# Rotating every filter group in float32 in place, and building the sine arguments on GpSimd, in a gated recurrence with a long convolution

## The chip, the cores and the metric

The kernel runs on one core of a Trainium2 chip. The metric is the device time of one execution in microseconds. Three runs of the kernel before gave 459.9, 460.58 and 461.4 us; the median is 460.58 us. The engines are called as in the profile: PE (TensorE, matrix products; PEld is its weight loading), DVE (VectorE), ACT (ScalarE), POOL (GpSimd) and SP (SyncE, which here only issues DMA transfers).

## The reference

Input `x` and `f_logit` have shape (4, 6272, 256): four sequences of 6272 steps with 256 channels. The first part is a gated linear recurrence, the second a convolution over the whole sequence between two projections, with multiplicative gates:

```
f = lower_bound + (1 - lower_bound) * sigmoid(f_logit);  i = 1 - f
h[t] = f[t] * h[t-1] + i[t] * x[t]                       # for all t
x1, x2, x3 = split(h @ w_proj, 3)                        # 256 -> 3 x 256
conv = irfft(rfft(x2, axis=time) * rfft(filter_fft, axis=time))   # circular, length 6272
out = (x1 * conv * x3) @ w_out
```

The filter is (6272, 256) and is the same for all four sequences, so its spectrum is needed once.

## The kernel before

The length 6272 is split as 49 x 128, and the transforms are done as two small dense transforms by matrix products. The tables for them (`D1`, `FT`, `VA`, `VB`, `ID`) are sines of arguments that are worked out on the chip from index tables.

**Stages.** `prepare` loads the filter, turns it into a spectrum and stores that in DRAM (`H`, 16 units). `hgrn(b)` loads `x` and `f_logit` of sequence b in 13 chunks, applies the sigmoid (ACT, L337), multiplies (POOL, L339), transposes on PE (L351), makes the gate (L364 or L366) and scans (DVE, L372) into `HA`. A copy of the beginning of `HA` behind its end, called a wrap, is made by ACT, POOL or a DMA (L301). `spectrum(b)` projects (`phase_p`, L725), does the first transform (L737), the second (L795), multiplies with the filter's spectrum (L816, L825) and goes back (L835). `gate(b)` forms x1 * x3 (L400, L422, L431); `phase_o(b)` finishes the inverse (L869), multiplies (L875), projects with `w_out` (L887) and stores. The projection of a batch reads every scan of that batch.

**The filter's way.** The 49 rows of 128 x 256 come in 13 groups: twelve of four rows (512 KB each) and one of a single row. Group g is loaded into a scratch place (`raws`: parts of the tiles X2, Hu and HA that later hold other things). A matrix product with a rotated identity, `rot`, turns each row by its own amount (`rotate`, L637); the result lies in two PSUM banks and is copied into the tile `f2` by ACT or DVE (operation `f2`, L291 or L296). All 13 copies must be there before the first transform of the filter, `FF1` (L661), which is followed by `afs` copies, `FF2` (L679), `hw` copies and stores (`hst`) for each of 16 units.

Before the change, six groups (`PLAIN`: 0, 2, 4, 6, 8, 10) are rotated as float32 straight from where the DMA put them. The other seven are first cast to float32r by ACT or POOL (operation `fr`) into one of two tiles (`afs` and `Hx`), and rotated from there. `rot` is a float32r tile that the plain groups read as float32.

**The sine arguments.** POOL writes eight index tables with iota (L512). DVE makes eleven columns of constants (one value a partition), multiplies and adds (L534, L537, L552), and folds the arguments into one period with two tensor-by-scalar passes and a subtraction (`fold`, L520 to L522), in two halves: `args0` for columns 0 to 519, `args1` for 520 to 1031. ACT takes the sine of each half (L563). Warming matmuls (`warm`, L603) fill gaps on PE.

**Order.** The functions do not issue anything; they record some 2,400 operations with what they read and write. The string `ORDER` then lists them all: three characters give the operation's number, its engine, and its PSUM bank. So the order on every engine, the choice of the engine, SP's queue of DMA issues and the PSUM banks are written out by hand (by an offline search that used the costs in the code). Each engine works through its list in order. An operation that must wait holds everything behind it on its engine. Eight PSUM banks of 512 float32 are shared by all; a rotation takes two, and a bank is free again when the copy that reads it has run.

```
def rotate(e, pb, r0=r0, rn=rn, fr=fr, turner=turner):
    pr = PS[:, pb:pb + 2].rearrange("m a (r e) -> m (a r) e", e=256)
    for r in range(r0, r0 + rn):
        nc.tensor.matmul(pr[:, r - r0, :], turner[:, m0_of(r):m0_of(r) + 128],
                         fr[:, r - r0, :], start=True, stop=True)
```

Of the kernel before, what the change touches and what calls it, by code (L numbers as in the profile page):

```python
# [21 lines left out]
S = 6272  # L22
# [13 lines left out]
PLAIN = (0, 2, 4, 6, 8, 10)  # L36
# [28 lines left out]
class Plan:  # L65
# [63 lines left out]
    "AAYBIgBFgAMYABIAgVACIA+gAkWBBgAhTBMgAvVAZVBWgArRBTgA9YANIAfRADgAiTAcSBPgBJAApXBKSAbQBLCBGQA/VBogBCYBagAPIAOABdgBHA"  # L129
    "BNSBhgBAFBkgBDWBOCDwgBUQAEYBXYDxgBEGARIEIgBQYAmVD8gBVABYVASIAlUATYBRTBZFD9gAVYAUIAdRAoQBbQBSLEJgBeABfSBcAEUgBiWBgK"  # L130
    "EVgBlAAeVBjOAQABmQBpAAxSBnAAqSBsYBqUAsXBrMAuXAFgBwUBuQAWYBxMB3WDyABvIB1UB4GBzSB2MByYDzYB+QEKAB0KB6UCAWB/AB7MD+ACFQ"
    "B5YD0SCBOCGACHUD1CD/YD4QCIED2KCDWEggD5ACKUB9gCEGD6IEhgEASELYCLEEEWEBKEsgEFGAjVECKCOQEtgEWAAtUAwUCCYCJYCVUAXYEGOCPA"
    "CXSCWEEMQAHACYKEQWEXYAJACQSE4gEROENAAyUE5gAaUCRKEiAESOCTSAIAAYYEYUCUCEOIEcWAKAFCgCeSCSYEZMEdGFDgEjYCgQCfCEeOChACaS"
    "EuACnQEaMEkWCZYCbCEvYCoIClUElGCjSE6AEmOEoQFMgCmECiYE7YEpIFNgCkCEwUEqICwWExEE0SCxGEyMCqQFXgETYE1CC1WErgCpYCrAEPYFWg"
    "E2KE8UEbYCNgFEAE/QC2OC3SFhgFAAFFYE9MCuWFggC4CCdgFBICvGAGgFOACzWE+MFGSCyYC0GC5YFPYFJQFHKC+UFqgFKAFIKEngC6WC/EFrgC7G"
    "FQUFLICtgDASFYADHWFRMAnRDBCFTQFSMDIGDCYDFSFZYF0gFUADQWB8gDGCFVIDDUFiAC9gDKSDEMFaQDRGDJYFjYDLCDXWFbIDVUALADNgDOSDYO"
    "DWEF1gFcIDPCFdWD7YFsADTUMTgDSYFeOCcgFkQDUEFtYDgSFfOFlAFnUDhCFmIDeWMfgFoEC8gDaSD3YDfGCMgFpMFuQEDYDbCMggDlWDZYCsgEfY"
    "F2AFvIDMgDnUDiYDmGEzYF+gDjSFwIDoEBtYFxWDkCE3YJQUFyODqQDpYJSEF3YFzOJRVDrAEHYJVSJWTJTFDsgF4QF7WJYDF5IDtgDuUJUYF8OJXC"
    "F6IF/gMUgJaTF9OGigJbQJZYJcDGIRJdIG0gDvEGQWJeYGJBG9gGUUGRGGGQDdgGVEGKSGHIMhAGAWGLCGOQGBOGMUGPAGrgGCSDcgGNEMrgGEQGDK"
    "MVAGSWGFAGWSGTOJfVGXCJgXJkRJlQJhFJmJGYTJnAJivGeVGZDJoYJpQJjYGfNJqXJuRJsHGaSJrIJwBGjWGbCJtYGcUGnuJvRGdEJzTJxpJ0QGoY"  # L140
    "J1DJ4XJyYJ2IGgSGsUJ6HGhKJ3YG1QGwEGluJ5XG5AHGSGkYJ7vGxYGmYJ9VHQgHHCJ+RGusJ8YGpWJ/FHMSGvYGqGG3oGtYHZgG+UG2YG6YKABHIW"
    "HNKG4YGyQHJGHAsHKSGzAKBYHigG7WHLCMsgHCsHBYKCQG/YMiYKEAHORHRTHDYHrgHPJMtAKDQHVrHERHTDKHVKFoG8GHWYHUYKITHFJKGYKMQKJF"
    "HaWKOAKKrH0UHeuKLYH4QHSYH+gH1EHbYHXSHcuHfYMuYHjUHYCHlsH5AHdYIHgH2WHgSH3GHnsHmYHkYHsQMWYHhCH6WHuoHoYIQgHpUH7GH/SHwo"
    "HvYHqEH8WKNQIBCH9OIIUHxYHtYIZgIDqIAYIRRIKEICYHyWITBKPoIEYKRTHzGIMsKQYKSUIiQKTDILYIsgIFWINYIjAKUsKWTIVpKVYKXVIGGMXQ"
    "IJYI1gKZFIUYKYLIWYIaWMYAMbUIeGMZIIOSM3gMcEM4gKbXISYIPCIfYMdMIXQKdHImSIYAIcuMjUInCIkQKaYMkMIdYJHgIoWIlAI+gKcTMlMIbY"
    "KgSIpGItQKerKiCIqUMnWIvoKfYIxAKhTNDgMoGIyYIgRIrMNEgIwYM5AMpOKlQI2UIhBKjrMvWI3YKnAIuYI6sKkYMzSM6YMwGKmRNQgI4EMxOKqQ"
    "I7YNPgM0CIzUKsAM1KM7WI0EJAYI5YNFAKrUKopKvSKtsKpYM8GM/QKuYKxCJIUNGYM9ONbgNAAI8SNcgJMEMygNBIKwXJKEK0WI9CI/UJLYKyvK2G"
    "K1RJBsKzYNHSK3BNRAK5WJDsJCYK4YNLQNICNlgK7OJEYJFUNMANSYNmgNJKK6XJGEK+WNdANNIK/SNTTJJYLAGNeYK8vNXQNUDLBqK9YLDVNvgNYA"
    "NVLLEWLCYNwgLFFLIXLKHLJVJNYLGuNnANfSLLtLHYLNWNZILMYLOXLPGNiUNgCLQvN5gJOQNjENhKLRYNoYNOgRtXJPAN6gRuWM+gNkMRvHLSQRwG"
    "LXSNxALTINpUNsWNqENyYLYKLUQODgNtGOEgNrMLZSLVAMeYNuOLcULWgLaCNaYNzQLdMLbgRyXN0ALhSR0HN1IN7AN2ULmWONgN3ELiKN8YOOgLeQ"  # L150
    "OFAN4MLjSLfALnOOGYLrULkCN9QLsMOAWN+ALoSMqAOXgN/IOYgOBGLlgOHULpCNKgOCOLwQOPAOKSLxILtWUwgOLCOQYLqgOIEOMKLyQLuGOJMLzA"
    "L1WORSOZAL2OL0gRzROSCOaYLvgL6UR1BNWYOTKOUQMaYObWM2YU8gL7MOVAL3SOcGNCAOdOOeUMmAOWIVJgL8WL4CVIgUxgOfMMEQL9GU9gOgML/S"
    "LggMFIOxUL5gL+gMAKOhQOyEOtWOiAOvTOuOUyAO3QOwDOjWO4AOnTUzYOkOVKAO1QOoDOpWO2AOlUU+AOzQOmMOrSU/YO0AMBUOsKOqGMJQMCEVLY"
# [43 lines left out]
def kernel(  # L197
# [241 lines left out]
    def prepare(head, tmp):  # L439
# [79 lines left out]
        def fold(a, b):  # L519
            ts(v[:, a:b], in0=w[:, a:b], scalar1=1.0 / S, scalar2=big, op0=AOP.mult, op1=AOP.add)  # L520
            ts(v[:, a:b], in0=v[:, a:b], scalar1=-big, scalar2=float(S), op0=AOP.add, op1=AOP.mult)
            dve.tensor_tensor(v[:, a:b], w[:, a:b], v[:, a:b], op=AOP.subtract)  # L522
# [455 lines left out]
```

## Time and profile before

| What | Value |
|---|---|
| median of three runs | 460.58 us |
| the profiled execution: its time, and its span on the core | 461.27 us, 459.3 us |
| PE busy | 444.2 us, 97% of the span |
| PE's weight loads | 346.6 us, 75% |
| DVE busy | 402.4 us, 88% |
| ACT busy | 406.7 us, 89% |
| POOL busy | 306.0 us, 67% |
| DMA moved | 121.40 MB, mean 264 GB/s |
| TensorE clock granted | 0.999 |

A row of groups reads: line, engine, operation, out<-in by tile names, shapes, xcount | busy us in total, mean ns of one | idle time of the engine just before, and what ended it. A row in order of time reads: start us, duration us, engine, line, operation, tiles, shapes, xcount [idle before <-releaser]. In the chain of waits, each row is a start, a duration and what it was. A busy PE means that matmuls are in flight, not that it runs at its peak. A line such as L291 or L296 is that of the helper `copy`, which many operations share; there the tile names tell what it is.

### The profile page before, as it was taken

How to read it: one execution, taken by the hardware profiler on the slowest of the kernel's cores; microseconds unless marked ns; L12 is line 12 of the kernel's file. 1: busy time of each engine (PE TensorE's matmuls, PEld its weight loads, DVE VectorE, ACT ScalarE, POOL GpSimd, SP SyncE). 2: the span in 40 equal slices, each digit the busy share in tenths (PEclk: the TensorE clock that was granted, in tenths of full speed). 3: DMA queues.
4: the chain of work that ended last, by engine and by line, in shares of the span. 5: the costliest groups of instructions: out<-in, count | busy, mean ns of one | idle time of the engine just before them, and what ended most of it. 6: DMA issues, size and time to landing. Idle time of an engine off the chain costs nothing.

```text
span 459.3 us, 14604 instructions
## 1 busy us (share of the span) xinstructions
PE 444.2 (97%) x6009; PEld 346.6 (75%) x6009; DVE 402.4 (88%) x450; ACT 406.7 (89%) x563; POOL 306.0 (67%) x282
## 2 busy tenths in 40 slices
PE   8999999999999999999999999999999999999996
PEld 6777777767766889878667789766768897777794
DVE  8389996699999995899999997999999976999873
ACT  6899999998999989989998978899999978898664
POOL 5399786288898743878897535979886504979500
PEclk9999999999999999999999999999999999999999
DMA  8999999848897998367769788399789750856077
GB/s 321 387 349 330 316 340 407 314 143 253 272 310 248 337 326 298 106 233 265 279 229 296 284 294 350 101 320 326 226 244 304 287 229 26 241 185 186 31 289 290
DMA packets 45154, 121.40 MB, mean 264 GB/s; under 512 B 4384, under 2 KB 8352, under 8 KB 45088
## 3 DMA queue, kind: packets, MB, share of 16 engines
q1 hardware_dynamic: 45088, 120.47, 75.2%
q8 instruction: 47, 0.77, 0.7%
q14 instruction: 19, 0.16, 0.1%
HBM read 86.12 MB, written 31.98 MB: 257 GB/s over the span
## 4 chain that ended last, share of the span: by engine, by line
PE 66%; DVE 15%; ACT 6%; DMA 5%; issue 5%; POOL 2%; ACTq 0%; SPq 0%; DVEq 0%; POOLq 0%
PE PS L400 15%; PE PS L725 9%; PE PS L835 9%; PE PS L887 7%; PE PS L351 6%; DVE HA L372 6%; PE PS L795 6%; PE PS L737 6%; DVE ys L875 4%; DMA FL<-in_f_logit_dram 3%; PE PS L869 2%; PE PS L661 2%; DVE PP L816 2%; DMA X<-in_moe_filter_fft_dram 1%; ACT fTs L364 1%
## 5 line engine op out<-in xcount | busy, mean ns | idle before, releaser
L339 POOL TENSOR_TENSOR XT<-XT,FL 128x1024 f32<-128x1024 f32 (+1 forms) x49 | 109.8, 2245 | 53.6 <-ACT FL L337 36.5
L372 DVE TENSOR_TENSOR_SCAN HA<-fTs,HA,PS 128x512 f16<-128x512 f32 (+1 forms) x96 | 112.9, 1201 | 2.8 <-ACT fTs L364 2.0
L400 PE MATMUL PS<-HA,W 128*128 128x490 f16 (+1 forms) x416 | 103.8, 367 | 1.0 <-DVE HA L372 0.3
L825 POOL TENSOR_TENSOR PP<-HA,Hu 98x1008 f16<-98x1008 f16 x39 | 81.8, 2106 | 6.8 <-ACT HA L291 2.7
L291 ACT CAST HA<-PS 128x1024 f16<-128x1024 f32 (+1 forms) x98 | 79.1, 833 | 4.2 <-PE PS L737 2.2
L431 POOL TENSOR_TENSOR zt<-gx 128x490 f16<-128x490 f32 (+1 forms) x43 | 52.4, 1223 | 41.1 <-ACT gx L291 16.6
L816 DVE TENSOR_TENSOR PP<-PS,Hu 98x1008 f16<-98x1008 f32 x57 | 66.7, 1199 | 0.6 <-ACT gx L293 0.5
L875 DVE TENSOR_TENSOR ys<-PS,zt 128x1024 fp32r<-128x1024 f32 (+1 forms) x52 | 58.7, 1149 | 8.5 <-PE PS L869 6.7
L887 PE MATMUL PS<-Wo,ys 128*128 128x256 f32 x392 | 58.1, 293 | 0.6 <-DVE ys L875 0.3
L364 ACT ACTIVATE fTs<-PS,cc 128x512 f32<-128x512 f32 (+1 forms) x84 | 55.3, 679 | 2.8 <-PE PS L351 2.1
L835 PEld LDWEIGHTS <-PP 98*128 98x128 f16 x1024 | 50.2, 97 | 9.8 <-issue 1.7
L400 PEld LDWEIGHTS <-W 128*128 128x128 f16 x416 | 34.4, 97 | 30.6 <-issue 7.8
L835 PE MATMUL PS<-VV,PP 98*128 98x98 f16 x1024 | 55.9, 206 | 0.3
L887 PEld LDWEIGHTS PS<-Wo,ys 128*128 128x128 f32 x392 | 49.7, 188 | 6.0 <-DVE ys L875 1.5
L293 ACT ACTIVATE gx<-PS 128x490 f32<-128x490 f32 (+1 forms) x87 | 50.1, 583 | 4.5 <-PE PS L400 3.1
L291 ACT CAST Th<-PS 128x784 f16<-128x784 f32 x59 | 48.4, 820 | 4.1 <-PE PS L835 3.1
L337 ACT ACTIVATE FL<-FL 128x1024 f32<-128x1024 f32 (+1 forms) x49 | 49.4, 1010 | 1.8 <-DMA FL<-in_f_logit_dram 1.6
L351 PE MATMUL PS<-iden,FL 64*128 64x64 f32 x736 | 42.7, 231 | 2.5 <-ACT HA L293 0.9
L725 PE MATMUL PS<-W,HA 128*128 128x256 f16 x392 | 44.6, 273 | 0.2
L725 PEld LDWEIGHTS <-HA 128*128 128x128 f16 x392 | 43.0, 142 | 1.2 <-issue 0.2
L351 PEld LDWEIGHTS PS<-iden,FL 64*128 64x128 f32 x736 | 31.7, 138 | 16.0 <-issue 2.6
L422 DVE TENSOR_TENSOR zt<-PS,gx 128x490 f16<-128x490 f32 (+1 forms) x61 | 38.8, 647 | 1.6 <-PE PS L400 0.9
(128 smaller groups left out, 741.8 us busy)
## 6 DMA issues: line engine op xcount, KB each, us to landing
FL<-in_f_logit_dram SPq DMA_DIRECT2D x45, 512.0 KB, 5.8
XT<-in_x_dram SPq DMA_DIRECT2D x45, 512.0 KB, 6.3
Hu<-H SPq DMA_DIRECT2D x39, 512.0 KB, 4.9
out_dram<-osb SPq DMA_DIRECT2D x22, 512.0 KB, 4.5
out_dram<-PP SPq DMA_DIRECT2D x16, 512.0 KB, 5.6
Hx<-H SPq DMA_DIRECT2D x13, 512.0 KB, 4.3
out_dram<-HA SPq DMA_DIRECT2D x10, 512.0 KB, 5.0
X<-in_moe_filter_fft_dram SPq DMA_DIRECT2D x9, 512.0 KB, 7.4
```

The lines of the kernel that those rows point to most:

```text
L291: nc.scalar.copy(dst, src)
L339: op("u", {"POOL": 0.1 + 0.553 * nb}, lambda e, xt=xt, ft=ft: nc.gpsimd.tensor_tensor(xt, xt, ft, op=AOP.mult), r=[("ft", k)], w=[("xt", k)])
L351: nc.tensor.transpose(bank(pb)[:, at[p] + j:at[p] + hn:nb], src[ps, j, cols], iden[ps, ps])
L364: nc.scalar.activation(fT, sT, AF.Identity, scale=by, bias=1.0)
L372: nc.vector.tensor_tensor_scan(h, fT, bank(pb)[:, 512 - hn:512 + hn], init, op0=AOP.mult, op1=AOP.add),
L400: nc.tensor.matmul(PS[:, p, 0:n], W13[:, kh, js], HA[:, HB[kh] + t0:HB[kh] + t0 + n], start=(kh == 0), stop=(kh == 1))
L725: nc.tensor.matmul(pp[:, r - r0, :], column(HB[kh], q_of(r)), W2[:, kh, :], start=(kh == 0), stop=(kh == 1))
L816: nc.vector.tensor_tensor(pr, px.unsqueeze(1).broadcast_to([TB, 2, UE, 63]), hh, op=AOP.mult)
L825: nc.gpsimd.tensor_tensor(pr, spec[:, o, :, 1:64].unsqueeze(1).broadcast_to([TB, 2, UE, 63]), hh, op=AOP.mult)
L835: nc.tensor.matmul(PS[:, ib + o, pr * TB:(pr + 1) * TB], PP[:TB, k, o, n, 2 * pr:2 * pr + 2, :], v[:TB], start=(n == 0), stop=(n == 1))
L875: nc.vector.tensor_tensor(late["ys"][:, yk, :, 0:rn * 128], PS[:, cb:cb + 2, 0:rn * 128], late["zt"][:].rearrange("p k r m -> p k (r m)") ...
L887: nc.tensor.matmul(po[:, i, :], late["ys"][:, yk, kh, i * 128:(i + 1) * 128], Wo[:, kh, :], start=(kh == 0), stop=(kh == 1))
```

## The change

1. `PLAIN` and the casts `fr` are gone. All 13 groups are rotated from where the DMA put them, as float32, and `rot` is a float32 tile. The cost written for a rotation, from which the order was searched, is 0.12 us a row for all of them, where it was 0.43 for a plain row and 0.12 for a cast one.
2. Three index tables are left of eight. The offsets that the other five held are now immediate scalars, so the five multiply-adds of the first half become eleven shorter ones.
3. The constant columns become an operation of their own on DVE (`cols`); both halves of the arguments run on POOL, in the order that is written.
4. `ORDER` is new throughout. On POOL the arguments stand behind the padding of `f2` and ahead of the table work. On ACT the list starts with the copy of group 0, the sine of the first half, and the copies of groups 2, 4, 6 and 3; the sine of the second half comes next. PE rotates groups 0, 1, 2, 4, 6, 5, 3, 8, 9, 7, 10, 12, 11; ACT runs the table load and first sigmoid after the copy of group 10, while DVE copies 12 and 11. Elsewhere some dozens of copies change engines, and wraps move to SP's queue: 27 of 48 are on it after, 18 before.

```diff
-PLAIN = (0, 2, 4, 6, 8, 10)
...
-        rot = tmp.tile([128, 256], F32R, name="rot")
+        rot = tmp.tile([128, 256], F32, name="rot")
...
-                    (128, [[0, 2], [49, 2], [98, 32]], 0), (128, [[1568, 2], [0, 64]], 1568),
-                    (98, [[0, 2], [2304, Q]], 0),
-                    (98, [[1568, 2], [0, Q]], 1568), (98, [[1568, 2], [0, Q]], 0),
-                    (98, [[-1568, 2], [0, Q]], 1568), (98, [[-1568, 2], [0, Q]], 3136),
-                    (256, [[49, 256]], 0)):
+                    (128, [[0, 2], [49, 2], [98, 32]], 0), (98, [[0, 2], [2304, Q]], 0), (256, [[49, 256]], 0)):
...
+        def folded(e):
+            g = pool if e == "POOL" else dve
+            def fold(a, b):
+                g.tensor_scalar(v[:, a:b], in0=w[:, a:b], scalar1=1.0 / S, scalar2=big, op0=AOP.mult, op1=AOP.add)
+                g.tensor_scalar(v[:, a:b], in0=v[:, a:b], scalar1=-big, scalar2=float(S), op0=AOP.add, op1=AOP.mult)
+                g.tensor_tensor(v[:, a:b], w[:, a:b], v[:, a:b], op=AOP.subtract)
+            return g, fold
...
-            stt(w[:, 0:128], in0=cD, scalar=prow[:], in1=oD, op0=AOP.mult, op1=AOP.add)
-            for i, k in enumerate((kre, kre, k2, k2)):
-                stt(w[:, 128 + 98 * i:226 + 98 * i], in0=cF, scalar=k,
-                    in1=oF[i], op0=AOP.mult, op1=AOP.add)
...
+        def args0(e):
+            g, fold = folded(e)
+            g.memset(cD[:, 64:65], 3136)
+            for at, n, c, k, o in [(0, 64, cD[:, 0:64], prow[:], 1568.0), (64, 1, cD[:, 64:65], prow[:], 1568.0),
+                                   (65, 63, cD[:, 65:128], prow[:], 3136.0)] + [
+                    (128 + 98 * i + Q * j, Q, cF[:, Q * j:Q * j + Q], k, o[j]) for i, (k, o) in enumerate((
+                        (kre, (1568.0, 3136.0)), (kre, (0.0, 1568.0)), (k2, (1568.0, 0.0)), (k2, (3136.0, 1568.0))))
+                    for j in range(2)]:
+                g.tensor_scalar(w[:, at:at + n], in0=c, scalar1=k, scalar2=o, op0=AOP.mult, op1=AOP.add)
+            fold(0, 520)
+
+        def args1(e):
+            g, fold = folded(e)
+            for i, (k, o) in enumerate(((kk, ore), (kim, oim))):
+                g.tensor_scalar(w[:, 520 + 256 * i:776 + 256 * i], in0=cI, scalar1=k, scalar2=o,
+                                op0=AOP.mult, op1=AOP.add)
             fold(520, 1032)
...
-            op("args", {"DVE": c}, fn, r=st + ["pint", "rot"] + ["cols0"] * i, w=[f"cols{i}", f"v{i}"])
+        op("cols", {"DVE": 1.7}, colset, r=["pint", "rot"], w=["cols1"])
+        for i, (fn, a, b, c, p) in enumerate(((args0, 0, 520, 4.5, 5.5), (args1, 520, 1032, 3.2, 3.2))):
+            op("args", {"DVE": c, "POOL": p}, fn, r=st + ["pint", "rot", "cols1"], w=[f"v{i}"])
...
-            if g in PLAIN:
-                fr, ft, turner = raw, et, rot[:].bitcast(F32)
-            else:
-                j = g // 2 % 2
-                fr, ft, turner = afs[j]...., [("af", j, 0), ("af", j, 1)], rot
-                op("fr", {"ACT": 0.08 + 0.214 * rn, "POOL": 0.1 + 0.235 * rn, "DVE": 0.1 + 0.267 * rn},
-                   lambda e, raw=raw, fr=fr, rn=rn: copy(e, fr[:, 0:rn], raw[:, 0:rn]), r=et, w=ft)
...
-            rt = op("rot", {"PE": (0.43 if g in PLAIN else 0.12) * rn}, rotate, r=ft + ["rot"], take=2)
+            rt = op("rot", {"PE": 0.12 * rn}, rotate, r=et + ["rot"], take=2)
```

More of the change, by code (lines that the diff above doesn't have):

```diff
@@ L134 @@
[L134 to L153, printed above, removed]
@@ L189 @@
[L189 to L192 removed]
+    "AAYA/gBCgAMYABIAaVACIBFgAbSBLgAuRBOgAnXA+YANIArSBRgAeTBIgAdSBXgAcUApQAwVAxXAOYBAWBBGBDQBEIBGSBjgBagBMQBUgBdgBggAQY"
@@ new lines @@
+    "APADqgBSVBHCDrgBNABPTBTFAvRD2gBQLAUYAsQECgBJQAWYATID3gBYWBKAAVIAyTARAADgAtVASIAzRBZGBbTEDgAXYBVQBcDBeWEOgBWABkSBhU"
+    "BlKAqTBiMBfGAiQAhQAgXAfTEPgAlRBoQBqSDsABvUBrKBxWBpABwMBtSBsYByGDtYD4AB4QBuKB6WB0UB7GB5IEEADuSB1MBzYAEYDyQDvCD5YB/W"
+    "EagDzICBUAFgDwKCAGEbgCCEB9WCEUD0IB+GB8YD6SEFYCFED7KD+WAmRD8KEngD/GCIQEmgCRUCDYCJAAYYEAOCPSEQAEGQCSMEcAEKWERYCKUEyg"
+    "ELOCQCB2gAIACLMEzgAKAEMOCNSEHABmYESUCOCEIIEWWE8gCYSEXGCMYCTYETMEdYE9gCaQAHAEYOCZCCbACUSEUMEoAChQEeWCVCEpYCiICfUEfO"
+    "E0AEiQCdSEgOFHgCgEFGgCeCCcYAkUCjYEjIEqUEhYAJAE1YCqWEkIErEENgEuSCrGEsMFQgCkQEvCCHgCvWClAFRgEwKE2UE+AE5QCwOCxSFagE6A"
@@ L193 @@
+    "kbOkeRiaYkfQkXqifVkhIkYYc/SkgJigFkcvkiYkjUkdYdACkoWkkMktQdBgkySkpOklUkqWkmEkuIkngk3UkrGkzKkvQk0WkwAk4Mk8Sk1Gkxgk5U"
+    "ksgk9Kk2glBWk6ElGSlCOk+Qk7glDUk/AlHKlLWlEElAglISlMOlFglQUlJClVWlRMlNQlKglSSlOAlWOlaUlTClPglXQlbMlUglYAlcWlZgA9VldO"
+    "A7QA5VA6QA8TlfSleglgKlhQliAljg"
 )
@@ L499, in prepare @@
         FTr = tmp.tile([128, 2, TB + Q], F32R, name="FTr")
-        cD, oD, cF, cI = ti[:, 0:128], ti[:, 128:256], ti[:, 256:354], ti[:, 746:1002]
-        oF = [ti[:, 354 + 98 * i:452 + 98 * i] for i in range(4)]
+        cD, cF, cI = ti[:, 0:128], ti[:, 128:226], ti[:, 226:482]
         def iotas(e):
@@ L514, in iotas, with colset @@
             pool.memset(FT[:], 0.0)
-        small(iotas, 1260, r=["iden"], w=st + ["pint", "FT"], e="POOL", kind="iota")
-        ts, stt, big = dve.tensor_scalar, dve.scalar_tensor_tensor, 12582912.0
[L519 to L522, printed above, removed]
-        def args0(e):
+        small(iotas, 740, r=["iden"], w=st + ["pint", "FT"], e="POOL", kind="iota")
+        big = 12582912.0
+        def folded(e):
[5 more added lines that the diff above has]
+            return g, fold
+        def colset(e):
+            ts, stt = dve.tensor_scalar, dve.scalar_tensor_tensor
             dve.tensor_copy(prow, pint)
@@ L550, in args1 @@
             ts(sgn, in0=sgn, scalar1=1.0, scalar2=None, op0=AOP.add)
-            for i, (k, o) in enumerate(((kk, ore), (kim, oim))):
-                ts(w[:, 520 + 256 * i:776 + 256 * i], in0=cI, scalar1=k, scalar2=o,
-                   op0=AOP.mult, op1=AOP.add)
             ts(odd, in0=kre, scalar1=18.0 / Q, scalar2=big, op0=AOP.mult, op1=AOP.add)
@@ L623, in prepare, with rotate @@
                 raw[:, 0:rn], ff[:, r0:r0 + rn, :]), w=et, dma=0.33 * rn, lag=2.6)
-            if g in PLAIN:
-                fr, ft, turner = raw, et, rot[:].bitcast(F32)
-            else:
-                j = g // 2 % 2
-                fr, ft, turner = afs[j].rearrange("m r i k -> m (r i k)").rearrange(
-                    "m (r d) -> m r d", d=D), [("af", j, 0), ("af", j, 1)], rot
-                op("fr", {"ACT": 0.08 + 0.214 * rn, "POOL": 0.1 + 0.235 * rn, "DVE": 0.1 + 0.267 * rn},
-                   lambda e, raw=raw, fr=fr, rn=rn: copy(e, fr[:, 0:rn], raw[:, 0:rn]), r=et, w=ft)
-            def rotate(e, pb, r0=r0, rn=rn, fr=fr, turner=turner):
+            def rotate(e, pb, r0=r0, rn=rn, raw=raw):
                 pr = PS[:, pb:pb + 2].rearrange("m a (r e) -> m (a r) e", e=256)
                 for r in range(r0, r0 + rn):
-                    nc.tensor.matmul(pr[:, r - r0, :], turner[:, m0_of(r):m0_of(r) + 128],
-                                     fr[:, r - r0, :], start=True, stop=True)
-            rt = op("rot", {"PE": (0.43 if g in PLAIN else 0.12) * rn}, rotate, r=ft + ["rot"], take=2)
+                    nc.tensor.matmul(pr[:, r - r0, :], rot[:, m0_of(r):m0_of(r) + 128],
+                                     raw[:, r - r0, :], start=True, stop=True)
+            rt = op("rot", {"PE": 0.12 * rn}, rotate, r=et + ["rot"], take=2)
             op("f2", either(256 * rn), lambda e, pb, r0=r0, rn=rn: copy(
```

104 lines of the change are left out of this document (55 added, 49 removed).

## The prediction

> **What bounds the kernel now.** I began with the busy time by stretch: the start (filter rotated), the rest of the first stage (filter spectra, gates and scans of batch 0), then its end.
>
> ```profile
> 0.00:23.60 23.60, 21.05 (x113) 16.46 (x113) 14.67 (x44) 17.33 (x18) 10.67 (x27) 1.00 0.93 355
> 23.60:72.00 48.40, 45.79 (x591) 36.65 (x592) 45.06 (x47) 47.66 (x68) 42.34 (x51) 1.00 0.94 337
> ```
>
> The columns are the stretch, its length, busy time of PE, PE's weight loads, DVE, ACT and POOL (instructions in brackets), granted clock, DMA share and GB/s. Up to 23.6 us no engine is full but PE is nearest (21.05). From there to 72 us ACT is the bound (47.66 of 48.4), DVE next with 3.3 us free. Second, the chain of waits, in order of time:
>
> ```profile
> 23.66 2.30 PE PS L661 x16
> ...
> 51.37 8.57 DMA FL<-in_f_logit_dram
> ...
> 75.32 10.70 PE PS L725 x98
> ...
> 245.56 6.86 DMA FL<-in_f_logit_dram
> ```
>
> Start and microseconds come first. The filter's first transform (L661) joins the chain at 23.66 us; by the code it reads all thirteen groups, so nothing of it can start before the last rotation (L637) is copied. The projection of batch 0 (L725) at 75.32 us is the next such barrier. The start of L661 is what the change moves.
>
> **The rotations.** Third, PE's own order of time:
>
> ```profile
> 1.36 4.01 PE L603 MATMUL PS<-iden 128*128 128x256 f16 x20 [1.36 <-POOL iden masks.py:199]
> ...
> 6.60 0.39 PE L603 MATMUL PS<-iden 128*128 128x256 f16 x2
> 6.83 5.35 PE L637 MATMUL PS<-X,rot 128*128 128x256 f32 x24
> 12.12 0.71 PE L637 MATMUL PS<-afs,rot 128*128 128x256 f32 x4
> ...
> 16.80 0.61 PE L603 MATMUL PS<-iden 128*128 128x256 f16 x4
> 17.25 1.89 PE L637 MATMUL PS<-Hu,rot 128*128 128x256 f32 x8
> ```
>
> Both types are printed as f32, but the source tile tells them apart: X and Hu are plain groups, afs holds a cast one. A plain group of 4 filter rows is eight matmuls, a cast group four: float32 runs each row as two instructions. Pitch, with start-up taken out by difference: (5.35 - 1.89)/16 = 0.216 us an instruction, so 0.432 us a plain row. A cast row is 0.71/4 = 0.178 us with the start-up left in. Before, 24 plain and 25 cast rows cost 24 x 0.432 + 25 x 0.178 = 14.8 us; after, 49 x 0.432 = 21.2 us: **at least 6.4 us more on PE**. The written cost of a float32 row falls from 0.43 to 0.12 in the diff, but the operation is the one that L637 already runs on X and Hu, so I take the trace's price. The new order was made for rotations that take a quarter of it.
>
> What goes:
>
> ```profile
> L291 ACT CAST Hx<-X 128x1024 fp32r<-128x1024 f32 x2 | 2.1, 1046 | 3.0 <-DMA X<-in_moe_filter_fft_dram 2.9
> L291 ACT CAST afs<-HA 128x1024 fp32r<-128x1024 f32 x1 | 1.0, 1045 | 0.9 <-DMA HA<-in_moe_filter_fft_dram 0.9
> L291 ACT CAST afs<-X 128x256 fp32r<-128x256 f32 x1 | 0.4, 388 | 0.0
> L303 POOL CAST afs<-X 128x1024 fp32r<-128x1024 f32 x2 | 2.1, 1042 | 3.0 <-DMA X<-in_moe_filter_fft_dram 2.9
> L303 POOL CAST Hx<-Hu 128x1024 fp32r<-128x1024 f32 x1 | 1.0, 1037 | 0.0
> ```
>
> Seven casts, 3.5 us of ACT and 3.1 of POOL. All lie before 23.6 us, where ACT has 6.3 us free; with PE as the limit they are worth nothing by themselves. At 355 GB/s a block of 512 KB (524 kB) lands every 1.48 us, PE now takes 4 x 0.432 = 1.73, so DMA does not set the pace either.
>
> **Sine arguments on POOL.** DVE loses them; DVE waits there anyway. POOL must finish the first half (520 columns) before ACT can take its sine, and in ACT's new order the copies of groups 2, 4 and 6 stand behind that sine. PSUM is eight banks; rotation 5 writes banks 3 and 4, bank 3 being held by group 2's copy. So PE can wait on POOL, at its sixth group. The rows for POOL and ACT, as groups and in order of time:
>
> ```profile
> L339 POOL TENSOR_TENSOR XT<-XT,FL 128x1024 f32<-128x1024 f32 x9 | 21.4, 2387 | 1.5 <-PE PS L661 0.9 <-ACT FL L337 0.5
> L291 ACT CAST f<-PS 128x1024 fp32r<-128x1024 f32 x9 | 10.2, 1157 | 1.6 <-PE PS L637 1.5
> L612 POOL CAST f<-iden 128x960 fp32r<-128x960 f32 x2 | 2.0, 1044 | 0.0
> L593 POOL TENSOR_SCALAR ID<-PP,cols 128x256 f16<-128x256 f32 x2 | 1.9, 947 | 0.0
> L512 POOL IOTA HA<- 128x98 int32 (+2 forms) x8 | 1.7, 251 | 0.0
> L563 ACT ACTIVATE PP<-PP 128x520 f32<-128x520 f32 (+1 forms) x2 | 1.3, 632 | 0.0
> L573 POOL TENSOR_SCALAR FTr<-PP,cols 128x49 fp32r<-128x49 f32 x2 | 0.8, 428 | 0.0
> ```
>
> ```profile
> 4.92 1.05 ACT L291 CAST Hx<-X 128x1024 fp32r<-128x1024 f32 x1 [2.90 <-DMA X<-in_moe_filter_fft_dram]
> 5.47 0.39 POOL L614 CAST f<-iden 128x16 fp32r<-128x16 f32 x1
> ...
> 8.78 1.04 POOL L303 CAST afs<-X 128x1024 fp32r<-128x1024 f32 x1 [2.92 <-DMA X<-in_moe_filter_fft_dram]
> 8.83 1.00 DVE L557 SCALAR_TENSOR_TENSOR cols<-cols 128x1 f32<-128x1 f32 x1
> ```
>
> Five of eight index tables go, about 0.23 us each (the mean is 0.251; the longest stays): POOL's padding then ends at 5.47 + 0.39 - 1.15 = 4.7 us. Eleven short operations of 49 to 64 columns lie between 0.251 (an index table's mean) and 0.428 (49 columns): I take 0.4, nearest in kind and size, 4.4 us. The fold has two one-input passes of 520, between 0.57 (the cast's 1.044 per 960) and 1.92 (0.947 per 256), taken at 1.3, as nothing lies closer, and one two-input pass, 2.387 x 520/1024 = 1.21. So the arguments end at 4.7 + 4.4 + 3.8 = 12.9 us (9.8 to 14.5), the sine at 13.6, group 2's copy at 14.7 (11.6 to 16.3). The second half, two products at 0.947 and a fold, follows by about 18.6, ahead of its sine behind group 3's copy. The column constants on DVE, twenty tiny operations, should be done by the padding's end; the last two rows above show a DVE operation on one column lasting 1.00 us while POOL casts 1024, so two casts of padding could hold them back by up to 2.1 us.
>
> The Trainium skill's page "GPSIMD Engine Reference" (section 3, Performance versus the Vector engine) gives a best case of 1.8 cycles an element for one input and about 2.6 for two, at 1.2 GHz: an estimate of 0.78, 0.78 and 1.13 us for the fold, by which POOL would be done 1.1 us sooner and PE would not wait. Its section 8 (Key points) says that GpSimd shares its SBUF interfaces with VectorE, in conflict with two-input or two-port DVE operations; the one-column row above agrees, and by that rule the constants do slip.
>
> **The sum.** Twenty-two warming matmuls come first: 1.36 + 4.01 x 22/20 = 5.77 us, when the first filter block has landed (ACT's wait for a first one ended at 4.92). Add 49 rows, 21.2; ten warming matmuls between them at (0.61 - 0.39)/2 = 0.11, 1.1; the wait for group 2's copy, 14.7 less the 5.77 + 5 x 1.73 = 14.4 when PE asks, 0.3; the last group's copy on DVE, about 1.3 with its hand-over. L661 starts near 29.7 us against 23.66: **6.0 us later** (5.7 to 7.6 by POOL's ends).
>
> What comes back: ACT finishes its last copy earlier than DVE and can do the table load and first sigmoid ahead of L661:
>
> ```profile
> 23.50 1.28 ACT L337 ACT_TABLE_LOAD   x1
> ...
> 24.80 1.06 ACT L337 ACTIVATE FL<-FL 128x1024 f32<-128x1024 f32 x1
> ```
>
> That is 2.3 us taken out of the ACT-bound stretch; moves of one f copy to DVE and one spectrum copy to ACT cancel. DVE can follow by at most its 3.3 us of slack and keeps its waits, so I count 1.3 us, between 0 and 2.3. **Net +4.7 us at the barrier of L725** (3.4 to 7.6).
>
> The rest of the order is new too. Wraps on SP's queue rise from 18 to 27, in batches 1 and 2 by eight; in batch 0 five gate copies move from ACT to DVE, and one output copy per later batch. The engine sums per batch hardly change, so I count zero, within 2 us either way, some three copies on PE's path. Nearest rows for a wait behind a late queue entry:
>
> ```profile
> SPq L334 <- PE PS L351: 10.2, 6, 3.6
> SPq L301 <- DVE HA L372: 4.0, 1, 4.0
> ```
>
> A wrap (L301) that waits for its scan holds every load queued behind it on SP, once for 4.0 us.
>
> The profiled execution took 461.27 us, 0.69 above the median of 460.58. 461.27 + 4.7 = 466.0; against the median 465.3.
>
> **Rivals.** *The delay is hidden*: the DMA wait of 8.57 us at 51.37 could set the end of the stage, so that L661 may slip for nothing: about 461, no change. For it: DMA share 0.94. Against it: loads wait for the transposes (L351) that free their buffers, 10.2 us in the rows above at batch 2, and those stand behind L661 on PE. 0.10.
> *Faster by the new order*: the wait of 6.86 us at 245.56 disappears, as its loads stand elsewhere in SP's queue: 465.3 - 6.9 = 458.4. It decides once later gains pass 4.7 us. Against: more wraps stand ahead of those loads. 0.09.
> *The float32 rotation is as cheap as its written cost*: at 0.178 us a row PE needs 8.7 us, the filter's landing decides again and some 2 us are won: 458.6. Rows L637 on X speak against it. 0.02.
> *POOL late*: the constants slip 2.1 us with the high prices, group 2's copy ends at 18.4, PE waits 4.0 instead of 0.3: 465.3 + 3.7 = 469. 0.13.
> *Wraps hold loads*: the 4.0 us wait again in a later batch, 469.3. 0.04.
>
> **How the numbers follow.** The forecast, 465.3 us (its own range 463 to 468), has 0.62. About 0.3% (1.4 us) is what a measurement can tell from no change. Slower: 0.62 + 0.13 + 0.04 = 0.79; within: 0.10; faster: 0.09 + 0.02 = 0.11. The range reaches to the hidden delay below and past the late cases above, 461 to 470.
>
> **What would show it.** Right: 98 matmuls at L637, all at 0.216 us pitch, ending near 28.4 us; L661 at 29 to 31; L725 near 80; no fr casts. Wrong: L637 with one instruction a row or L661 before 26; POOL's arguments ending after 16; L725 back at 75 to 77; or a gap against before that shrinks after batch 0.

## The result and the profile after

The changed kernel took 466.62 us (median of four runs, 466.21 to 467.49); the kernel before, run beside it on the same chip, took 460.24. The recorded ratio is 1.0129 with a 95% interval of 1.0105 to 1.0152: slower by 1.3%, which is 5.9 us (the two medians are 6.4 us apart; the sum forecast 4.7). The profiled execution shown here took 466.7 us, its span 464.6, where before it was 461.27 and 459.3.

Line numbers moved with the change: rotation is L630 (was L637), the filter's first transform L654 (L661), the projection L718 (L725), warming L605, the copies L290 and L292 on ACT and L295 on DVE.

The chain of waits of the changed kernel (start us, duration us, what), the rows that answer to those shown before, and the rotations ahead of them:

```profile
5.55 10.36 PE PS L630 x48
16.35 3.46 PE PS L630 x16
20.46 7.35 PE PS L630 x34
29.28 2.12 PE PS L654 x16
...
51.12 7.28 DMA FL<-in_f_logit_dram
...
81.29 10.72 PE PS L718 x98
...
130.74 7.46 DMA XT<-in_x_dram
...
266.99 1.87 DMA FL<-in_f_logit_dram
```

The rotations themselves are now on the chain, almost without a break from 5.55 to 27.8 us. The first transform starts at 29.28 where it started at 23.66 (+5.6). The loads that held batch 0 at 51.37 us for 8.57 us do so at 51.12 for 7.28. Of the long DMA wait at 245.56 only 1.87 us is left (at 266.99), but another of 7.46 us stands at 130.74.

PE's use of `rot`, by source tile (min, median and longest of one instruction in ns, first and last start in us):

```profile
L630 PE MATMUL PS<-X,rot x74: 379/379/382, 5.4 to 27.4; 128*128 128x256 f32 x74
L630 PE MATMUL PS<-Hu,rot x16: 379/379/379, 17.9 to 23.5; 128*128 128x256 f32 x16
L630 PE MATMUL PS<-HA,rot x8: 379/379/382, 20.3 to 21.8; 128*128 128x256 f32 x8
```

74 + 16 + 8 = 98, two instructions for each of 49 rows. The 379 ns are the time from start to end of one, and the next starts before that; the pitch comes from the rows below. The start of the changed kernel in order of time:

```profile
2.60 1.97 POOL L614 CAST f<-iden 128x960 fp32r<-128x960 f32 x2
2.68 0.95 DVE L532 SCALAR_TENSOR_TENSOR cols<-cols 128x1 f32<-128x1 f32 x1
3.66 0.93 DVE L533 SCALAR_TENSOR_TENSOR cols<-cols 128x1 f32<-128x1 f32 x1
...
4.85 1.07 POOL L553 TENSOR_SCALAR HA<-HA,prow 128x64 f32<-128x64 int32 x3
...
5.39 10.53 PE L630 MATMUL PS<-X,rot 128*128 128x256 f32 x48
...
5.99 3.00 POOL L553 TENSOR_SCALAR HA<-HA,cols 128x49 f32<-128x49 int32 x8
...
9.08 0.62 POOL L517 TENSOR_SCALAR PP<-HA 128x520 f32<-128x520 f32 x1
9.79 0.62 POOL L518 TENSOR_SCALAR PP<-PP 128x520 f32<-128x520 f32 x1
...
10.50 1.29 POOL L519 TENSOR_TENSOR PP<-HA,PP 128x520 f32<-128x520 f32 x1
...
11.82 0.64 ACT L565 ACTIVATE PP<-PP 128x520 f32<-128x520 f32 x1 [2.05 <-POOL PP L519]
12.36 3.22 ACT L290 CAST f<-PS 128x1024 fp32r<-128x1024 f32 x3
...
14.37 1.28 POOL L519 TENSOR_TENSOR PP<-HA,PP 128x512 f32<-128x512 f32 x1
...
16.19 1.89 PE L630 MATMUL PS<-X,rot 128*128 128x256 f32 x8
...
26.86 1.28 ACT L336 ACT_TABLE_LOAD   x1
27.91 1.23 DVE L295 CAST f<-PS 128x1024 fp32r<-128x1024 f32 x1 [1.18 <-PE PS L630]
28.16 1.06 ACT L336 ACTIVATE FL<-FL 128x1024 f32<-128x1024 f32 x1
```

PE runs 48 rotations in one row with no wait in brackets. ACT waits 2.05 us for POOL's arguments, and PE does not notice. The table load and first sigmoid run ahead of the first transform.

Busy time by stretch: the filter's start (the same 18.2 us in both), and from the first transform to the projection of batch 0. Columns as in the prediction. Before, then after:

```profile
5.40:23.60 18.20, 17.04 (x93) 13.75 (x93) 10.81 (x29) 15.57 (x17) 5.87 (x10) 1.00 1.01 395
23.70:75.20 51.50, 48.82 (x617) 38.19 (x618) 47.40 (x51) 50.28 (x73) 44.23 (x53) 1.00 0.95 342
```

```profile
5.40:23.60 18.20, 18.20 (x92) 15.88 (x91) 3.38 (x8) 10.14 (x10) 11.00 (x24) 1.00 1.03 410
29.30:81.10 51.80, 48.72 (x612) 37.58 (x613) 48.46 (x52) 47.87 (x70) 41.92 (x46) 1.00 0.84 296
```

In the start PE has become the bound (18.20 of 18.20); of ACT, DVE and POOL none is busy for more than 11.0 us of it. The DMA engines are as full after as before (share 1.03 and 1.01), but no row of PE's rotations waits for them after the change. In the second stretch ACT lost 2.4 us of work, as the prediction said, and the stretch is as long as before (51.8 against 51.5). What did not change there is the amount of PE's work (48.8 and 48.7).

The gap in the start of each batch's projection (before 75.16, 171.51, 272.74, 371.73 us; after 81.13, 177.72, 278.45, 377.05) is +5.97, +6.21, +5.71 and +5.32, and the spans differ by 5.3. The loss is complete at 29 us; little is added or given back later. The 0.65 us by which the gap shrinks from batch 0 to batch 3 is less than two executions of the same kernel differ (459.42 to 461.4 us before).

### The profile page after: what moved, and what is told of

The parts are those of the page before. It is cut to its first block, busy times and chain, and to the rows that moved or that the text cites. A ratio compares the mean times of both kernels' runs of the same rounds, so it can differ in the third digit from the quotient of the medians.

```text
span 464.6 us, 14648 instructions
## 1 busy us (share of the span) xinstructions
PE 450.7 (97%) x6034; PEld 352.7 (76%) x6034; DVE 402.5 (87%) x444; ACT 397.0 (85%) x548; POOL 306.0 (66%) x286
## 4 chain that ended last, share of the span: by engine, by line
PE 66%; DVE 14%; ACT 6%; POOL 5%; issue 4%; DMA 4%; DVEq 0%; SPq 0%; ACTq 0%; POOLq 0%
PE PS L399 14%; PE PS L718 9%; PE PS L880 8%; PE PS L828 7%; DVE HA L371 5%; PE PS L730 5%; PE PS L788 5%; PE PS L350 5%; PE PS L630 5%; DVE ys L868 4%; PE PS L862 3%; POOL XT L338 3%; DMA FL<-in_f_logit_dram 2%; PE PS L654 2%; DMA XT<-in_x_dram 2%
## 5 line engine op out<-in xcount | busy, mean ns | idle before, releaser
L399 PE MATMUL PS<-HA,W 128*128 128x490 f16 (+1 forms) x416 | 102.7, 367 | 1.3 <-DVE HA L371 0.8
L290 ACT CAST HA<-PS 128x1024 f16<-128x1024 f32 (+1 forms) x96 | 78.2, 837 | 6.1 <-PE PS L730 2.7
L818 POOL TENSOR_TENSOR PP<-HA,Hu 98x1008 f16<-98x1008 f16 x38 | 79.8, 2107 | 5.0 <-ACT HA L290 2.6
L809 DVE TENSOR_TENSOR PP<-PS,Hu 98x1008 f16<-98x1008 f32 x58 | 68.0, 1199 | 0.0
L290 ACT CAST Th<-PS 128x784 f16<-128x784 f32 x59 | 48.3, 821 | 6.1 <-PE PS L828 4.3
L292 ACT ACTIVATE gx<-PS 128x490 f32<-128x490 f32 (+1 forms) x84 | 48.3, 584 | 2.4 <-PE PS L399 1.5
L718 PE MATMUL PS<-W,HA 128*128 128x256 f16 x392 | 44.5, 273 | 0.2
L718 PEld LDWEIGHTS <-HA 128*128 128x128 f16 x392 | 42.9, 142 | 1.2 <-DVE HA L371 0.3
L290 ACT CAST X<-PS 128x1024 f16<-128x1024 f32 (+1 forms) x31 | 32.6, 1092 | 9.8 <-PE PS L718 8.5
```

The costliest lines, as they stand in the source:

```text
L290: nc.scalar.copy(dst, src)
L399: nc.tensor.matmul(PS[:, p, 0:n], W13[:, kh, js], HA[:, HB[kh] + t0:HB[kh] + t0 + n], start=(kh == 0), stop=(kh == 1))
L718: nc.tensor.matmul(pp[:, r - r0, :], column(HB[kh], q_of(r)), W2[:, kh, :], start=(kh == 0), stop=(kh == 1))
L809: nc.vector.tensor_tensor(pr, px.unsqueeze(1).broadcast_to([TB, 2, UE, 63]), hh, op=AOP.mult)
L818: nc.gpsimd.tensor_tensor(pr, spec[:, o, :, 1:64].unsqueeze(1).broadcast_to([TB, 2, UE, 63]), hh, op=AOP.mult)
```

## The experiments

Theory A is the prediction's: rotations in float32 take PE 0.25 us more a row, all of it ahead of the first transform. Rivals: B, the arguments on POOL cost the time; C, the new order does; and for the recovery that did not come, D, ACT or DVE paces the stretch after the filter, or E, PE does. In the table "first" is the start of the filter's first transform, "projection" that of batch 0, both in the profiled execution (us). Each ratio is to the kernel before as it ran beside that kernel, with medians of 460.24 us (after), 461.08 (e1 to e4), 461.12 (e5 to e7) and 460.80 (e8 to e10); compare ratios, not medians.

| Kernel | first | projection | between | median us | ratio to before, 95% |
|---|---|---|---|---|---|
| before | 23.66 | 75.16 | 51.50 | 460.24 | |
| after | 29.28 | 81.13 | 51.85 | 466.62 | 1.0129 [1.0105, 1.0152] |
| e1_plain | 30.39 | 81.59 | 51.20 | 466.05 | 1.0106 [1.0089, 1.0123] |
| e2_args_dve | 29.37 | 80.73 | 51.36 | 467.14 | 1.0131 [1.0116, 1.0146] |
| e3_casts_back | 24.22 | 76.02 | 51.80 | 461.95 | 1.0023 [1.0008, 1.0038] |
| e4_tables | 30.56 | 81.82 | 51.26 | 467.05 | 1.0129 [1.0107, 1.0151] |
| e5_f_on_act | 30.40 | 83.00 | 52.60 | 468.70 | 1.0162 [1.0142, 1.0182] |
| e6_mend (e3's kernel again) | 24.31 | 75.68 | 51.37 | 462.46 | 1.0027 [1.0010, 1.0044] |
| e7_half | 26.24 | 77.84 | 51.60 | 463.09 | 1.0042 [1.0029, 1.0055] |
| e8_more_pe | 30.39 | 85.47 | 55.08 | 470.21 | 1.0200 [1.0177, 1.0224] |
| e9_no_fill | 29.97 | 81.14 | 51.17 | 467.58 | 1.0145 [1.0127, 1.0164] |
| e10_before_no_fill | 23.81 | 75.16 | 51.35 | 460.42 | 0.9992 [0.9979, 1.0005] |

**The float32 rotation alone (e1_plain).** The kernel before, its own order and its arguments on DVE, with every group plain.

```diff
-PLAIN = (0, 2, 4, 6, 8, 10)
+PLAIN = tuple(range(13))
 # ORDER: the seven fr entries dropped, nothing else moved
```

> The kernel before with one part of the change alone: all thirteen groups rotated in float32 where they land, no casts, every engine's list otherwise as before; the sine arguments stay on DVE. If the float32 rotations are the cause, PE's 98 rotation matmuls at 0.216 us end near 28.5 us, the filter's first transform starts at 29 to 30 us instead of 23.7, and the time is 465 to 467 us, nearly that of the changed kernel. If the new order or the arguments on POOL are the cause, the first transform moves by less than 2 us and the time stays at 460 to 462 us.

It has most of the loss by itself: 1.0106, and the first transform at 30.39, later than the 29 to 30 us expected; 1.2 us of that is a late change of PE's pace in this execution (last section). PE at its end, in order of time:

```profile
29.00 0.60 PE L637 MATMUL PS<-X,rot 128*128 128x256 f32 x2
29.43 0.60 PE L603 MATMUL PS<-iden 128*128 128x256 f16 x4
30.39 2.23 PE L661 MATMUL PS<-D1r,f 128*128 128x256 f32 x16 [0.36 <-DVE f L296]
```

The last rotation is one plain row at 29.00, and the transform follows one copy behind it.

**The casts put back (e3_casts_back).** The changed kernel, with the seven casts and float32r rotations again; six of the casts on DVE, one on ACT, so that ACT and POOL keep their new lists.

```diff
+PLAIN = (0, 2, 4, 6, 8, 10)
...
-        rot = tmp.tile([128, 256], F32, name="rot")
+        rot = tmp.tile([128, 256], F32R, name="rot")
...
+            if g in PLAIN:
+                fr, ft, turner = raw, et, rot[:].bitcast(F32)
+            else:
+                fr, ft, turner = afs[j]...., [("af", j, 0), ("af", j, 1)], rot
+                op("fr", {"ACT": 0.08 + 0.214 * rn, "POOL": 0.1 + 0.235 * rn, "DVE": 0.1 + 0.267 * rn},
+                   lambda e, raw=raw, fr=fr, rn=rn: copy(e, fr[:, 0:rn], raw[:, 0:rn]), r=et, w=ft)
 # ORDER: + fr of groups 1, 5, 3, 7, 12, 11 on DVE, of group 9 on ACT
```

> The changed kernel with the seven casts and the float32r rotations of these groups put back (six casts on DVE, which idles there, one on ACT); new order and arguments on POOL otherwise kept. If the float32 rotations are the cause, the first transform goes back to 23.5 to 25.5 us and the time to 460 to 462 us. If the rest of the new order is the cause, the time stays above 465 us.

The loss falls from 1.29% to 0.23%. This and e1 come at the change from its two ends and add up: 1.06 + 0.23 = 1.29 (so exactly by luck, since each is known to within 0.15 or 0.17%). So float32 rotation without casts is 4.9 us of it (1.06% of 460.24; 4.1 to 5.7 by the interval) and the rest of the change, with the casts on DVE as here, 1.1 us (0.4 to 1.8). In this kernel the arguments on POOL do cost a wait. ACT, then PE, in order of time:

```profile
12.59 0.64 ACT L566 ACTIVATE PP<-PP 128x520 f32<-128x520 f32 x1 [2.56 <-POOL PP L520]
...
14.30 0.75 PE L640 MATMUL PS<-afs,rot 128*128 128x256 f32 x4 [1.08 <-ACT f L291]
...
24.22 2.15 PE L664 MATMUL PS<-D1r,f 128*128 128x256 f32 x16
```

PE, faster here, meets the copy that stands behind ACT's sine and waits 1.08 us for it; in the changed kernel PE is too slow to meet it.

**Half of the dose (e7_half).** The kernel before with three more plain groups: 36 plain rows and 13 cast ones.

```diff
-PLAIN = (0, 2, 4, 6, 8, 10)
+PLAIN = (0, 2, 4, 5, 6, 7, 8, 9, 10)
 # ORDER: three fr entries dropped
```

> The kernel before with three more groups (5, 7, 9) rotated in float32 without a cast, so 36 plain rows and 13 cast ones; all else as before. If PE is the limit, each row changed costs about 0.25 us beyond the slack of the start: the first transform begins at 26 to 27.2 us, half way to the run with all rows plain, and the time is 463 to 464.5 us. If a few plain rows are hidden by the filter's landing, the first transform begins before 25 us and the time stays within 1.4 us of the kernel before.

```profile
25.07 0.36 PE L637 MATMUL PS<-afs,rot 128*128 128x256 f32 x1
...
26.24 2.30 PE L661 MATMUL PS<-D1r,f 128*128 128x256 f32 x16
```

With 24, 36 and 49 plain rows in the order of before, the first transform starts at 23.66, 26.24 and 30.39: 0.22 us a row over the first twelve, 0.32 over the next thirteen (0.23 without the 1.2 us of e1's late change of pace, told in the last section). The forecast had 0.432 - 0.178 = 0.254.

**The arguments back on DVE (e2_args_dve).**

```diff
 # ORDER, both args operations
-POOL
+DVE
```

> The changed kernel with both halves of the sine arguments on DVE, at the same place of the order. If POOL's part costs nothing because PE is the limit up to the first transform, that transform stays at 29.3 us within 0.3 and the time within 0.7 us of the changed kernel's 466.6 us. If ACT's wait of 2.05 us for POOL reaches PE through the PSUM banks, the first transform comes up to 0.5 us earlier and the time falls to about 466.0 us.

DVE and then PE, in order of time:

```profile
6.16 1.32 DVE L553 TENSOR_SCALAR HA<-HA,cols 128x49 f32<-128x49 int32 x8
...
29.37 2.14 PE L654 MATMUL PS<-D1r,f 128*128 128x256 f32 x16 [0.17 <-DVE f L295]
```

DVE does the eight 49-column operations in 1.32 us where POOL took 3.00, and the first transform does not come sooner (29.37 against 29.28). Ratio 1.0131 against 1.0129: B falls for this kernel, since PE covers POOL's arguments.

**What paces the stretch after the filter (e4, e5, e8, e9, e10).** The prediction took ACT for the bound and counted 1.3 us back when it was relieved. The stretch did not shrink, so each neighbour was tried. First two pieces of table work moved up in POOL's list, to the end of the work that it does ahead of the first transform (e4):

```diff
 # ORDER on POOL
-rest0, ..., rest1, ..., rest2 (ID)
+rest0, rest1, rest2 (ID), ...
```

> The changed kernel with two table operations of POOL (the second rest of the tables and the inverse table ID, 3.5 us together) moved from the middle of the ACT-bound stretch into POOL's idle 13.7 us before the first transform. If POOL's queue is what kept the 1.3 us from coming back, the projection of batch 0 starts at 78.5 to 80.2 us instead of 81.1 and the time falls to 464 to 465.8 us. If POOL only follows the loads and transposes, the projection stays at 81 us within 0.4 and the time at 466.6 us within 0.5.

Nothing: 1.0129. The ID table is then done by 23 us, ahead of the first transform, the stretch is 51.26 us, where e2, with these operations left in it, has 51.36, and POOL is not what holds it. (The projection is late, at 81.82, because the first transform was, at 30.56.) Then four gate copies of batch 0 from DVE to ACT (e5). The change had moved two of them, 1 and 8, the other way; 14 and 19 were on DVE before it too:

```diff
 # ORDER: gate copies f 1, 8, 14, 19 of batch 0
-DVE
+ACT
```

> The changed kernel with four gate copies of batch 0 (chunk halves 1, 8, 14 and 19) moved from DVE to ACT, which has 3.2 us free between the first transform and the projection, while DVE has 1.8. If DVE's load is what kept the freed 2.3 us of ACT from shortening that stretch, it falls from 51.9 us to 49.5 to 51 us and the time to 464 to 466 us. If the chain through PE's order and the PSUM banks sets it, the stretch stays at 51.2 to 52 us and the time at 466 to 467.3 us.

The stretch of e5 by engine:

```profile
30.40:83.00 52.60, 48.47 (x612) 37.61 (x613) 45.77 (x48) 49.61 (x74) 42.03 (x46) 1.00 0.83 292
```

Neither expectation came: the stretch (52.60) and the time (468.70) lie above both. (By the row of the changed kernel ACT had 3.9 us free there and DVE 3.3, not 3.2 and 1.8.) DVE is relieved by 2.7 us (45.77 against 48.46), ACT loaded by 1.7, and the stretch is 0.75 us longer: DVE alone was not the bound, and work added to ACT does cost something. Yet ACT's relief by 2.4 us in the change itself, with 1.1 us more for DVE, gave nothing. So I gave PE more to do: sixteen pairs of warming matmuls, one pair ahead of each second transform (e8), and in e9 took the stretch's own four warming operations out, to the end of the kernel. e10 does the same to the kernel before with its six.

```diff
-WARM = 36
+WARM = 52
 # ORDER, e8: + one warm (two matmuls) ahead of each FF2
 # ORDER, e9: warm 12, 10, 9, 14 moved behind the last operation
 # ORDER, e10 (before): warm 10, 20, 23, 25, 1, 14 moved behind the last operation
```

> The changed kernel with sixteen more pairs of warming matmuls, one ahead of each second transform of the filter: about 0.22 us of PE each, 3.5 us in all, between the first transform and the projection of batch 0. If PE's list paces that stretch, it grows from 51.9 us to 54 to 55.5 us and the time to 468.5 to 470.5 us. If ACT or DVE paces it, PE has 3 us of gaps to hide them in: the stretch stays under 52.7 us and the time within 1 us of 466.6.

> The changed kernel with the four pairs of warming matmuls that stand in the same stretch moved behind the last operation of the kernel: about 0.9 us of PE taken away there. If PE's list paces the stretch, it falls to 50.9 to 51.5 us and the time by 0.4 to 0.9 us. If they only fill waits, nothing moves beyond 0.3 us.

> The kernel before with its six pairs of warming matmuls of that stretch moved behind the last operation: about 1.3 us of PE. If PE's list paces the stretch, it falls from 51.5 us to 50.2 to 51 us and the time by 0.5 to 1.3 us, which would beat both kernels. If they only fill waits, the time stays within 0.4 us of the kernel before.

The same stretch in e8, then in e9:

```profile
30.40:85.50 55.10, 52.76 (x645) 39.73 (x646) 48.81 (x52) 48.44 (x70) 41.97 (x46) 1.00 0.82 281
```

```profile
30.00:81.10 51.10, 47.60 (x604) 37.05 (x605) 48.26 (x52) 47.77 (x70) 41.85 (x46) 1.00 0.85 300
```

In e8 4.04 us more of PE's busy time made the stretch 3.23 us longer and the kernel 3.3 us slower (ratio 1.0200 against 1.0129), with no more instructions for any other engine. In e9 1.12 us less made it 0.68 shorter than in the changed kernel; but e2 and e4, with the same lists of PE, ACT and DVE in this stretch, have 51.36 and 51.26, so that this is not clear of what executions differ by, and the time is not better (1.0145 against 1.0129, with intervals that overlap). In e10 the stretch stays (51.35 against 51.50) and the time is level with before.

The traces show where the relief goes. These are the longest of PE's waits in the stretch (who waited for whom: us in total, times, longest), before and then after:

```profile
PE PS L679 <- ACT afs L291: 1.0, 2, 0.7
PE PS L679 <- DVE afs L296: 0.3, 1, 0.3
```

```profile
PE PS L672 <- ACT W L482: 0.9, 1, 0.9
PE PS L672 <- ACT afs L290: 0.7, 1, 0.7
```

| Kernel | stretch | PE busy | PE's waits for ACT, sum | for DVE, sum |
|---|---|---|---|---|
| before | 51.50 | 48.82 | 1.9 | 0.5 |
| after | 51.85 | 48.72 | 2.4 | 0.4 |
| e5_f_on_act | 52.60 | 48.47 | 3.7 | 0.2 |
| e8_more_pe | 55.08 | 52.76 | 1.2 | 1.1 |
| e9_no_fill | 51.17 | 47.60 | 2.5 | 0.9 |
| e10_before_no_fill | 51.35 | 48.03 | 1.5 | 1.2 |

PE's work and its waits together make up the stretch to within 0.7 us. Less work for ACT can only shorten PE's waits for it, 1.9 us before the change, and it did not shorten them; less work for PE came back in part as longer waits (2.8 to 3.4 us in e9, 2.4 to 2.7 in e10). E stands in part: PE's list, with its waits for the copies of ACT and DVE, paces this stretch, and work added to it is paid at four fifths (3.23/4.04) or more. That ACT has no part in it is not shown, since work added to ACT lengthened PE's waits for it (e5); nor is it shown that taking work from PE makes the kernel faster.

**e3 a second time (e6_mend).** This was to be e3 with the first sine behind group 4's copy on ACT, so that the copy of group 2 no longer waits for POOL, and with e5's moves. The kernel that ran under this label has neither: it is e3's, line for line.

> The changed kernel with the casts and float32r rotations of seven groups back, the first sine moved behind group 4's copy on ACT (so that no copy waits for POOL), and the same four gate copies moved to ACT. If both waits matter, the first transform starts at 22.8 to 23.9 us and the time is 458.5 to 460.5 us, a little under the kernel before. If the filter's landing sets the start and PE's chain the rest, the first transform stays at 23.7 to 24.3 us and the time at 461 to 462 us.

So this expectation was not tested, and whether such a mend gains anything is open. The sine still stands ahead of the copies on ACT:

```profile
12.65 0.64 ACT L566 ACTIVATE PP<-PP 128x520 f32<-128x520 f32 x1 [1.73 <-POOL PP L520]
13.19 4.49 ACT L291 CAST f<-PS 128x1024 fp32r<-128x1024 f32 x4
```

What the run gives is e3 measured again, on another chip: 1.0027 against 1.0023, the first transform at 24.31 against 24.22, the stretch 51.37 against 51.80. The last pair tells how far two executions of one kernel differ there. The profiled execution took 465.56 us, far over its median, and its clock stood at half for 3.4 us (granted 0.57 between 266 and 270 us), long after the rows used here. No variant beat the kernel before; the best is e10, level with it.

## Why the prediction was right

The time came within the range and on the side given, 1.3 us above the forecast (466.62 against 465.3). The cause, float32 rotations on PE ahead of the first transform, is shown by e1, e3 and e7. One term of the sum failed, the recovery.

**Rotations: right.** The pitch after is (10.53 - 1.89)/40 = 0.216 us, the figure taken from before. The last rotation ends at 23.76 + 4.05 = 27.8 us (28.4 forecast), the first transform starts at 29.28 (29.7): 5.6 us later than before instead of 6.0. The Trainium skill ("FP8 and Floating Point Precision", Matmul Precision) says that true float32 takes four passes through the array. The rows agree: 0.432 us a row of 256 columns, 3.9 times the 0.11 us of a 256-column warming matmul in f16.

**Casts worth nothing: not quite.** Before, PE waited for two of them, in all 0.92 us:

```profile
6.02 0.74 PE L637 MATMUL PS<-Hx,rot 128*128 128x256 f32 x4 [0.64 <-ACT Hx L291]
15.14 0.74 PE L637 MATMUL PS<-Hx,rot 128*128 128x256 f32 x4 [0.28 <-POOL Hx L303]
```

These waits went with the casts. The sum has this without naming it, since it lets PE rotate from 5.77 us on with no wait for a cast. They are about what lies between the 6.4 us of extra rotation and the 5.6 us by which the first transform slips.

**Arguments on POOL: right in effect, high in price.** Forecast to end at 12.9 us, they ended at 11.79; group 2's copy ends near 13.4, not 14.7, and PE does not wait. The one-input passes took 0.62 us each (1.3 taken, the middle of wide bounds, was twice too much), the two-input pass 1.29 (1.21 taken), the 49-column operations 0.375 (0.4). The prediction's estimate for the fold from the Trainium skill ("GPSIMD Engine Reference", section 3), 0.78, 0.78 and 1.13 us, sums to 2.7 and the rows to 2.5; against it the one-input passes are a fifth shorter and the two-input pass a seventh longer. The two constant operations beside POOL's casts took 0.95 and 0.93 us, so the constants did slip; but POOL's first three argument operations read `prow` alone, and the eight that read the constants follow them at 5.99 us without a wait. The POOL-late rival's 2.1 us cost nothing.

**Recovery: the step that failed.** "2.3 us taken out of the ACT-bound stretch ... I count 1.3 us." ACT's work did go (50.28 to 47.87 us of the stretch), and nothing came back: the stretch is 51.85 us against 51.50, a difference within what executions of the same lists show (51.26 to 51.85). ACT had the highest busy time there by a little, but what could come back was only PE's waits for it, 1.9 us before, and these did not shrink (2.4 after, 2.1 in e2, 2.0 in e4); e8 shows that work on PE's list sets the pace. In these traces the step was off by 1.65 us (1.3 + 0.35); the first transform, 0.4 earlier than summed, happened to take some of that back, which leaves the +5.97 us at the barrier against the +4.7 of the sum.

**The rest of the order: within its bounds.** Counted at zero, within 2 us. By e3 the order and the arguments together cost 1.1 us (0.4 to 1.8). Half of it, 0.56 us, shows in e3 as a later start of the first transform (24.22 against 23.66); that the wait for POOL is the reason was not tested, and the remainder was not traced.

**Rivals.** "Faster by the new order": its mechanism came, since the wait at 245.56 fell from 6.86 to 1.87 us, but one of 7.46 us appeared at 130.74, and the gap at the batches' starts moved by less than 1 us. "The delay is hidden": the wait at 51 us shortened by 1.3 us only. "Wraps hold loads": no gap grew after batch 1.

## What to carry to other kernels

When a tile is no longer cast, the cost that goes is on the casting engine and the cost that comes is on PE; look for a row of the old trace that already runs the uncast form, take its pitch from the difference of two counts, and do not believe a cost table that the order was searched with. An engine with the highest busy share in a stretch is not yet its bound: read what the others wait for, then load and relieve one engine at a time, and see which of them moves the stretch. A barrier that reads every product of a loop passes on the delay of the last one in full.

## What the runs showed of the hardware beyond that

PE starts each execution at half its pace, for a time that differs from one execution to the next, and the granted clock of 1.00 in a row does not show it. In every trace the early warming matmuls start 0.213 us apart and later ones 0.109; float32 rotations that fall into the first part start 0.427 us apart instead of 0.216. In e4 they do, and 22 warming matmuls take 4.87 us (4.19 in the changed kernel) and the first 48 rotations 11.17 (10.53):

```profile
1.36 4.87 PE L605 MATMUL PS<-iden 128*128 128x256 f16 x22 [1.36 <-POOL iden masks.py:199]
6.03 11.17 PE L630 MATMUL PS<-X,rot 128*128 128x256 f32 x48
...
30.56 2.12 PE L654 MATMUL PS<-D1r,f 128*128 128x256 f32 x16 [0.17 <-DVE f L295]
```

The pace changes where the trace's own record of the clock begins, and the views count the time ahead of that as full clock. The record begins at 4.71 us after, 4.79 before, 4.89 in e2, 6.13 in e9, 6.99 in e5 and e8, 7.22 in e1 and 7.33 in e4; the twelve traces lie between 4.43 and 7.33. Where PE waits for no other engine, half of the delay reaches the first transform. In e4 the pace changes 2.62 us later than after and the first transform starts 1.28 later; in e5 it is 2.28 and 1.12, in e9 1.42 and 0.69, in e2 0.18 and 0.09. On the same ground 1.2 us of e1's 30.39 is of this kind ((7.22 - 4.79)/2), which leaves 29.2. Where PE does wait, the delay is hidden: the kernel of e3 and e6 changed pace at 5.22 and at 7.04 us, and its first transform starts at 24.22 and 24.31, with a wait for ACT's copy of 1.08 and 0.30 us. So of two kernels bound by PE at the start, compare the pace of the warming matmuls first. What sets the time of the change is not shown here.
